# Ten spreading products cut into a product step and a read step, and gate and val converted in another order at the start

## Chip, cores and metric

One core of one Trainium2 chip runs the whole program. The metric is the device time of one execution in microseconds (us), the median over runs. Engines are called as in the profile: PE (TensorE, matmul), DVE (VectorE), ACT (ScalarE), POOL (GpSimd), SP (SyncE, which starts the DMAs here).

## What is computed

Attention of 4 x 8 heads over 576 positions with head size 64, where half of the heads look at the last 32 positions and half at every 32nd; then two feed-forward layers over the 2304 tokens. The inputs are float32, and the output is wanted to float32's accuracy.

```python
attn_out = _attn_ref(q, k, v)
x = attn_out.transpose(0, 2, 1, 3).reshape(B * S, H * D)   # 2304 x 512
h = x @ w_in                                               # 512 -> 2048
x = (h * np.cos(h)) @ w_out                                # 2048 -> 512
g = x @ w_gate                                             # 512 -> 1536
out = (g * (1.0 / (1.0 + np.exp(-g))) * (x @ w_val)) @ w_out2
```

## The kernel before

Every float32 matmul of the two layers is done as three float16 matmuls on a high and a low part of each operand (`mm3`, lines 559 to 561 in the profile). The parts are cut after the operand was multiplied by a scale that is common to a whole matrix or to a block of tokens. Weights arrive as 512 KB tiles of eight-byte words (`raw`, loaded from line 174 on SP's queue); ACT converts with line 233, DVE with lines 240 and 244, POOL joins with line 936 for the second layer's gate and val; then the high part is cut on ACT (line 254) and the low part on DVE (line 257), and finished tiles of the second layer are stored to DRAM (line 882).

A common scale takes three things. Partial maxima per partition are made while data passes by (lines 183 and 537). `spread_tops` (lines 120 to 137, DVE) makes of them a diagonal matrix, the `tops`. `common_scale` (lines 139 to 145) multiplies it on PE by a matrix of ones into a `bank` (line 142, the *spreading product*, 128 columns for each matrix or block), so that each partition sees all maxima, takes the maximum from the bank on DVE (line 143, the *read*) and makes the scale (lines 116 to 118). There are ten such products in an execution: for the matrices in, out, gate with val, and out2; for the first layer's input block 0, block 1, and blocks 2 to 4 together; and for the second layer's input block 0, blocks 1 to 3, and block 4.

A `bank` is one of four buffers in PSUM, which products and up-projections share; a new one is the buffer that was given back first.

The tokens are cut into five blocks, three of 512 and two of 384. The first layer runs in slots, one for each block and each of 16 tiles m of the hidden size. In a slot the program issues, in this order:

- PE: the up-projection of (block, m), twelve matmuls into a bank (`up1`), then the down-projections that are due, twelve matmuls each into four accumulators `acc` (`contract`). No down stands in the first 14 slots; later they catch up with the ups;
- ACT: the a step of this slot (line 592); DVE: the b step of the slot before (line 595);
- ACT and POOL finish an older slot's hidden tile (lines 606, 607);
- one piece of the `urgent` list (maxima, scales and splits of the token blocks);
- half of the slot's budget of `later` work (weights: maxima, tops, scales, conversions, each with a cost in us);
- ACT: the c step (line 599) and DVE: the d step (line 602), which reads the bank for the last time and so gives it back;
- the other half of the budget.

At the end of a block the accumulators are stored by ACT (line 575) and DVE (line 573) in `store_scaled`. Every engine works off its own instructions in the order in which the program issued them, so a step's place in the lists above decides what waits behind it. The steps that the change touches are put on the lists at these places: `scale_pieces` (token blocks, line 533 on), `direct_later` (matrix out), `open_weights` (gate with val, and out2, once enough of the hidden buffers are free), and `pair_half`, which sets the order of the conversions of gate and val. XM is the m of block 0 at which the urgent pieces of block 1 are listed.

Of the kernel before, what the change touches and what calls it, by code (L numbers as in the profile page):

```python
# [43 lines left out]
TW_IN = 2.0 ** 10  # L44
TW_OUT = 2.0 ** 14
TW_LAST = 2.0 ** 13
# [9 lines left out]
HEAD, HSHARE = 14, 0.8  # L56
RATE, MINLAG = 0.4, 2
RAW = 6
XM = 5
HOMES, LATE, UNIT, FREE = 24, 4, 16, 12  # L60
W7S = 3
SHARE, SHARE2, SB = 0.95, 0.85, 2
# [17 lines left out]
def build(tc, qk_l, qk_s, v_l, v_s, w_in, w_out, w_gate, w_val, w_out2, mask_l, mask_s, eye32, eye16, out):  # L80
    nc = tc.nc
    wide = w_in.dtype != F32
    with ExitStack() as ctx:
# [13 lines left out]
        ones16 = small.tile([128, 128], BF16, name="ones16")  # L97
# [9 lines left out]
        def brief(name, n=1):  # L107
            return small.tile([128, n], F32, name=f"{name}{n}", bufs=2)
# [27 lines left out]
                nc.vector.tensor_scalar(out=d[:, i], in0=id16, scalar1=p[:, i:i + 1], scalar2=None, op0=ALU.mult)  # L136
            return d

        def common_scale(d, bound, n=1):

            t, p = bank()[:, 0:128 * n].rearrange("p (n c) -> p n c", n=n), brief("q", n)
            nc.tensor.matmul(out=t, lhsT=ones16, rhs=d, start=True, stop=True)
            nc.vector.tensor_reduce(out=p, in_=t, op=ALU.max, axis=AX.X)
            s, inv = finish_scale(p, bound, n)
            return [(s[:, i:i + 1], inv[:, i:i + 1]) for i in range(n)]
# [14 lines left out]
        scale_w = {}  # L160
# [27 lines left out]
        def later(cost, fn, key=None):  # L188
            fill.append((cost, fn, key))
# [102 lines left out]
        tops = {}  # L292
# [3 lines left out]
            parts = parts_two if len(mats) == 2 else parts_w[mats[0]]  # L296
            later(0.6, lambda: tops.__setitem__(mats, spread_tops(parts, wide, len(mats))))

        def set_scales(bound, *mats):
            scale_w.update(zip(mats, common_scale(tops[mats], bound, len(mats))))  # L300

        def scale_later(bound, *mats):
            later(0.6, lambda: set_scales(bound, *mats))

        rests = deque()

        def direct_later(mat, j, tiles):

            box, steps = conv_steps(mat, j, lambda: ring.tile([128, 512], F32, name="cv", bufs=3), False)
            if rests:  # L310
                steps.append(rests.popleft())
            if j == 0:
                steps.append((0.6, lambda: set_scales(TW_OUT, mat)))
            steps.append((0, lambda: hi_part(tiles[j][:, 0], box["c"], scale_w[mat][0])))
            begin(steps)
            rests.append((0.7, lambda: lo_part(tiles[j][:, 1], box["c"], scale_w[mat][0], tiles[j][:, 0]), (mat, j)))
# [106 lines left out]
        def bank():  # L423
            return pm.tile([128, 512], F32, name="bank")
# [103 lines left out]
        def scale_pieces(blks, scales, at_once=1):  # L528
            n = len(blks)
            parts = cols("parts", n * (KC + 1)).rearrange("p (n k) -> p n k", n=n)  # L530
            box = {}
            nc.gpsimd.memset(parts[:, :, KC:], TINY)
            todo = [(i, k) for i in range(n) for k in range(KC)]

            def piece(some):
                for i, k in some:
                    nc.vector.tensor_reduce(out=parts[:, i, k:k + 1], in_=xy[blks[i]][:, k, :], op=ALU.max, axis=AX.X,
                                            apply_absolute_value=True)
            for i in range(0, len(todo), at_once):
                yield 0.65 * at_once, lambda some=todo[i:i + at_once]: piece(some)  # L540
            yield 0.6, lambda: box.__setitem__("top", spread_tops(parts if n > 1 else parts[:, 0], False, n))
            yield 0.6, lambda: scales.update(zip(blks, common_scale(box["top"], TX, n)))

        def split_pieces(blk, scales, dst):
# [235 lines left out]
                later(cost, fn)  # L780
        top_later("in")
        scan_later("out", 0)
        scale_later(TW_IN, "in")
        split_chain([("in", j, wi) for j in range(M1)], 2, lambda j: scan_later("out", j + 1) if j + 1 < M1 else top_later("out"))

        for i in range(2):
# [1 line left out]
        steps = deque()  # L788
# [5 lines left out]
        for k in range(len(gs) + LAGS[3] + 1):  # L794
            def group(lag):
                return gs[k - lag] if 0 <= k - lag < len(gs) else None
            i, g = 2 * (k // 6), k % 6
# [117 lines left out]
        def pair_half(j, mi, mat, last, ahead):  # L915
# [31 lines left out]

            g = [conv_steps(mat, 2 * j + q, lambda q=q: place(q), False)[1] for q in range(2)]
            his, los = ahead
            for step in (g[0][0:1] + los[0:1] + g[0][1:] + his[1:2] + g[1][0:1] + his[2:3] + g[1][1:2] + los[1:2] + g[1][2:]  # L950
                         + his[3:] + los[2:] + [(0, lambda k=k: combine(k)) for k in range(4)] + [(0, lambda: hi(0))]):
                if step:
                    later(*step)
            return [(0, lambda q=q: hi(q)) for q in range(3)], [(0.95, lambda q=q: lo(q)) for q in range(3)]

        def open_weights(lag):

            if lag + 4 <= FREE:
                most[0] = FREE
            if not opened and most[0] == FREE and max(taken, default=0) < FREE:  # L960
                opened.append(True)
                scale_later(TW_IN, "gate", "val")
                pairs_later()
                later(0, lambda: None, "pairs")
                for i in range(M2):
                    scan_later("out2", i, 0.8)
                top_later("out2")
            if len(opened) == 1 and lag < LATE and max(taken, default=0) < LATE:
                opened.append(True)
                most[0] = LATE  # L970
                for i in range(3):
                    later(1.0, lambda: None)
                scale_later(TW_LAST, "out2")
                seven_later()

        opened, most = [], [HOMES]
# [366 lines left out]
```

## Time and profile before

| what | value |
|---|---|
| runs, us | 881.54, 884.5, 879.95 (median 881.54) |
| the profiled execution | 880.38 us, span 878.6 us |
| mean granted TensorE clock | 0.992 |
| DVE busy | 658.8 us (75%) |
| ACT busy | 522.0 us (59%) |
| POOL busy | 202.5 us (23%) |
| DMA | 200.58 MB, 66.5% of 16 engines' span on the main queue |

The span runs from the first to the last instruction of the profiled execution, and its time has 1.8 us around it. Busy time counts an instruction from its start to its (for PE: modelled) end. The attention takes about the first 112 us with the first weights beside it, the first layer runs to about 500 us, the second to the end. The spreading products run at 63.8, 86.3, 131.1, 139.0, 217.0, 243.9, 381.0, 414.1, 485.4 and 648.7 us.

### The profile page before, as it was taken

What the parts mean: (1) busy time and instruction counts of PE and PEld (TensorE: products, weight loads), DVE (VectorE), ACT (ScalarE), POOL (GpSimd) and SP (SyncE); (2) the same over time, 40 slices, a digit from 0 to 9 for tenths busy, and PEclk for the clock granted to TensorE, in tenths of its full rate; (3) what the DMA queues carried; (4) which work ended last, traced back from release to release, by engine and by line L of the source; (5) the groups of instructions that cost most, each with busy time, mean ns of one, the idle gap of its engine ahead of it and who ended that gap; (6) DMA issues with size and microseconds to landing.
All of it is one profiled execution on the core that took longest, in us unless ns stands there. A gap on an engine that the chain in (4) does not pass through costs nothing.

```text
span 878.6 us, 18390 instructions
## 1 busy us (share of the span) xinstructions
PE 851.0 (97%) x7223; PEld 604.9 (69%) x7223; DVE 658.8 (75%) x1256; ACT 522.0 (59%) x1046; POOL 202.5 (23%) x249
## 2 busy tenths in 40 slices
PE   7999999999999999999999998999999999999998
PEld 4776644444444444455656687888888899999998
DVE  5898989995788989979997378657766765765562
ACT  4888989762556767567886365554444534544440
POOL 3343324221245567323223100000000000000000
PEclk8899999999999999999999999999999999999999
DMA  9998842566855565734546147576777778898894
GB/s 296 358 312 256 268 166 73 167 191 241 288 179 186 175 213 206 257 151 136 198 147 226 69 168 275 195 263 226 264 244 249 250 241 282 296 321 296 321 326 157
DMA packets 53510, 200.58 MB, mean 228 GB/s; under 512 B 5456, under 2 KB 16208, under 8 KB 49584
## 3 DMA queue, kind: packets, MB, share of 16 engines
q1 hardware_dynamic: 53424, 199.42, 66.5%
q8 instruction: 56, 0.92, 0.4%
q14 instruction: 30, 0.25, 0.1%
HBM read 175.41 MB, written 23.99 MB: 227 GB/s over the span
## 4 chain that ended last, share of the span: by engine, by line
PE 74%; issue 6%; POOL 6%; DVE 5%; DMA 4%; ACT 4%; SPq 0%; POOLq 0%; ACTq 0%; DVEq 0%
PE acc L712 14%; PE bank L559 12%; PE bank L561 11%; PE bank L560 11%; PE acc L559 6%; PE acc L561 6%; PE acc L560 6%; POOL arena L936 3%; PE bank L448 2%; POOL arena L607 2%; PE po L501 2%; DMA vl<-v_l 1%; DMA v_pair<-v_s 1%; DVE arena L257 1%; ACT tb L592 1%
## 5 line engine op out<-in xcount | busy, mean ns | idle before, releaser
L559 PE MATMUL bank<-xs,wi 128*128 128x256 f16 (+3 forms) x780 | 232.6, 298 | 12.2 <-DVE tb L602 7.2
L561 PE MATMUL bank<-xs,wi 128*128 128x256 f16 (+3 forms) x780 | 232.6, 298 | 0.0
L560 PE MATMUL bank<-xs,wi 128*128 128x256 f16 (+3 forms) x780 | 232.6, 298 | 0.0
L607 POOL TENSOR_TENSOR arena<-tb,arena 128x512 f16<-128x512 f32 (+1 forms) x80 | 94.1, 1176 | 234.0 <-ACT arena L606 213.8
L560 PEld LDWEIGHTS <-wi 128*128 128x128 f16 x880 | 86.0, 98 | 51.3 <-issue 17.9
L559 PE MATMUL acc<-arena 128*128 128x512 f16 (+1 forms) x320 | 114.5, 358 | 0.0
L560 PE MATMUL acc<-arena 128*128 128x512 f16 (+1 forms) x320 | 114.5, 358 | 0.0
L561 PE MATMUL acc<-arena 128*128 128x512 f16 (+1 forms) x320 | 114.5, 358 | 0.0
L559 PEld LDWEIGHTS <-wi 128*128 128x128 f16 x880 | 86.1, 98 | 35.1
L561 PEld LDWEIGHTS <-wi 128*128 128x128 f16 x880 | 86.1, 98 | 34.8
L712 PEld LDWEIGHTS <-arena 128*128 128x128 f16 x1080 | 100.7, 98 | 8.1
L697 POOL TENSOR_TENSOR wi<-tb 128x256 f32<-128x256 f32 (+1 forms) x30 | 20.2, 673 | 341.7 <-DVE tb L679 341.7
L679 DVE SCALAR_TENSOR_TENSOR tb<-tb,c,arena 128x512 f32<-128x512 f32 (+1 forms) x60 | 41.6, 693 | 63.5 <-ACT tb L674 63.4
L560 PEld LDWEIGHTS <-arena 128*128 128x128 f16 x600 | 58.7, 98 | 34.1 <-issue 1.4
L712 PE MATMUL acc<-arena 128*128 128x256 f16 (+1 forms) x702 | 82.0, 265 | 0.0
L561 PEld LDWEIGHTS <-arena 128*128 128x128 f16 x600 | 58.7, 98 | 32.8
L559 PEld LDWEIGHTS <-arena 128*128 128x128 f16 x600 | 58.7, 98 | 32.6
L592 ACT ACTIVATE tb<-bank,quarter,c 128x512 int32<-128x512 f32 (+1 forms) x75 | 54.4, 725 | 39.0 <-PE bank L561 28.2
L682 ACT ACTIVATE arena<-tb 128x256 f16<-128x256 f32 (+3 forms) x59 | 28.9, 489 | 79.7 <-DVE tb L679 79.7
L1211 DVE TENSOR_TENSOR arena<-bank,cv 128x512 f32<-128x512 f32 (+1 forms) x60 | 38.1, 635 | 45.8 <-PE bank L561 45.2
L606 ACT ACTIVATE arena<-tb 128x512 f16<-128x512 f32 (+1 forms) x80 | 46.6, 583 | 37.6 <-PE acc L561 35.1
L559 PE MATMUL bank<-xs,arena 128*128 128x256 f16 (+1 forms) x240 | 62.9, 262 | 1.2 <-DVE arena L1211 1.2
(144 smaller groups left out, 1711.9 us busy)
## 6 DMA issues: line engine op xcount, KB each, us to landing
wi<-w SPq DMA_DIRECT2D x20, 1792.0 KB
arena<-w SPq DMA_DIRECT2D x60, 576.0 KB, 5.2
raw<-w_out SPq DMA_DIRECT2D x56, 512.0 KB, 4.3
arena<-w SPq DMA_DIRECT2D x10, 1792.0 KB
raw<-w_gate SPq DMA_DIRECT2D x24, 512.0 KB, 4.1
raw<-w_val SPq DMA_DIRECT2D x24, 512.0 KB, 4.8
w<-arena SPq DMA_DIRECT2D x42, 256.0 KB, 2.8
raw<-w_in SPq DMA_DIRECT2D x16, 512.0 KB
```

The costliest lines, as they stand in the source:

```text
L559: nc.tensor.matmul(out=o, lhsT=w[:, 0, c], rhs=x[0], start=first, stop=False, **kw)
L560: nc.tensor.matmul(out=o, lhsT=w[:, 0, c], rhs=x[1], start=False, stop=False, **kw)
L561: nc.tensor.matmul(out=o, lhsT=w[:, 1, c], rhs=x[0], start=False, stop=last, **kw)
L592: nc.scalar.activation(out=c["w"].bitcast(I32), in_=c["ph"], func=AF.Identity, scale=turn[c["blk"]], bias=quarter)
L606: nc.scalar.activation(out=g[:, 0, 0:n], in_=w, func=AF.Copy)
L607: nc.gpsimd.tensor_tensor(out=g[:, 1, 0:n], in0=w, in1=g[:, 0, 0:n], op=ALU.subtract)
L679: nc.vector.scalar_tensor_tensor(out=t, in0=t, scalar=s_g[c["blk"]], in1=c["C"][m][:, 1, 0:c["n"]], op0=ALU.mult, op1=ALU.mult)
L682: nc.scalar.activation(out=to, in_=src, func=AF.Copy, scale=2.0 ** -11)
L697: nc.gpsimd.tensor_tensor(out=t_sums[:, 0, 0:h], in0=c["t"][0][:, h:2 * h], in1=c["t"][0][:, 0:h], op=ALU.subtract)
L712: nc.tensor.matmul(out=o[:, c], lhsT=w[:, 256 * i + 128 * c:256 * i + 128 * c + 128], rhs=unit(u)[:, x:x + h], start=j == c == i == 0, sto ...
L936: nc.gpsimd.tensor_tensor(out=out, in0=a, in1=b, op=op)
L1211: nc.vector.tensor_tensor(out=c["C"][m][:, :, h * right:h * right + h], in0=p, in1=t, op=ALU.add)
```

## The change

`common_scale` loses its product, which becomes `spread_product`. Where a scale was one step of a list (product and read together, cost 0.6), there are now two: the product at cost 0, then, as the next step of the list, the read with the scale at cost 0.6. For the urgent list, which gives one piece to a slot, that is the next slot. For out2 the three empty steps of cost 1.0 ahead of the scale become one ahead of the product and two between product and read. For gate and val the step leaves `open_weights`; the product is issued first in the conversions of the first half pair, whose conversions follow it at once, and the read stands behind the first conversions of the second half. XM goes from 5 to 4, and the list of block 1 has one step more.

```diff
--- before.py
+++ after.py
@@ -56,7 +56,7 @@
 HEAD, HSHARE = 14, 0.8
 RATE, MINLAG = 0.4, 2
 RAW = 6
-XM = 5
+XM = 4
 HOMES, LATE, UNIT, FREE = 24, 4, 16, 12
 W7S = 3
 SHARE, SHARE2, SB = 0.95, 0.85, 2
@@ -136,10 +136,13 @@
                 nc.vector.tensor_scalar(out=d[:, i], in0=id16, scalar1=p[:, i:i + 1], scalar2=None, op0=ALU.mult)
             return d
 
-        def common_scale(d, bound, n=1):
-
-            t, p = bank()[:, 0:128 * n].rearrange("p (n c) -> p n c", n=n), brief("q", n)
+        def spread_product(d, n=1):
+            t = bank()[:, 0:128 * n].rearrange("p (n c) -> p n c", n=n)
             nc.tensor.matmul(out=t, lhsT=ones16, rhs=d, start=True, stop=True)
+            return t
+
+        def common_scale(t, bound, n=1):
+            p = brief("q", n)
             nc.vector.tensor_reduce(out=p, in_=t, op=ALU.max, axis=AX.X)
             s, inv = finish_scale(p, bound, n)
             return [(s[:, i:i + 1], inv[:, i:i + 1]) for i in range(n)]
@@ -296,11 +299,11 @@
             parts = parts_two if len(mats) == 2 else parts_w[mats[0]]
             later(0.6, lambda: tops.__setitem__(mats, spread_tops(parts, wide, len(mats))))
 
-        def set_scales(bound, *mats):
-            scale_w.update(zip(mats, common_scale(tops[mats], bound, len(mats))))
-
-        def scale_later(bound, *mats):
-            later(0.6, lambda: set_scales(bound, *mats))
+        def product_step(*mats):
+            return 0, lambda: tops.__setitem__(mats, spread_product(tops[mats], len(mats)))
+
+        def scale_step(bound, *mats):
+            return 0.6, lambda: scale_w.update(zip(mats, common_scale(tops[mats], bound, len(mats))))
 
         rests = deque()
 
@@ -310,7 +313,8 @@
             if rests:
                 steps.append(rests.popleft())
             if j == 0:
-                steps.append((0.6, lambda: set_scales(TW_OUT, mat)))
+                steps[1:1] = [product_step(mat)]
+                steps.append(scale_step(TW_OUT, mat))
             steps.append((0, lambda: hi_part(tiles[j][:, 0], box["c"], scale_w[mat][0])))
             begin(steps)
             rests.append((0.7, lambda: lo_part(tiles[j][:, 1], box["c"], scale_w[mat][0], tiles[j][:, 0]), (mat, j)))
@@ -539,6 +543,7 @@
             for i in range(0, len(todo), at_once):
                 yield 0.65 * at_once, lambda some=todo[i:i + at_once]: piece(some)
             yield 0.6, lambda: box.__setitem__("top", spread_tops(parts if n > 1 else parts[:, 0], False, n))
+            yield 0, lambda: box.__setitem__("top", spread_product(box["top"], n))
             yield 0.6, lambda: scales.update(zip(blks, common_scale(box["top"], TX, n)))
 
         def split_pieces(blk, scales, dst):
@@ -780,7 +785,8 @@
                 later(cost, fn)
         top_later("in")
         scan_later("out", 0)
-        scale_later(TW_IN, "in")
+        later(*product_step("in"))
+        later(*scale_step(TW_IN, "in"))
         split_chain([("in", j, wi) for j in range(M1)], 2, lambda j: scan_later("out", j + 1) if j + 1 < M1 else top_later("out"))
 
         for i in range(2):
@@ -947,6 +953,16 @@
 
             g = [conv_steps(mat, 2 * j + q, lambda q=q: place(q), False)[1] for q in range(2)]
             his, los = ahead
+            if j == 0:
+                first = g[0] + g[1] + [(0, lambda k=k: combine(k)) for k in range(4)]
+                if mi == 0:
+                    for step in [product_step("gate", "val")] + first:
+                        later(*step)
+                    return [(0, lambda q=q: hi(q)) for q in range(3)], [(0.95, lambda q=q: lo(q)) for q in range(3)]
+                for step in (g[0] + [scale_step(TW_IN, "gate", "val")] + his[0:1] + g[1][0:1] + his[1:2] + g[1][1:2] + los[0:1]
+                             + his[2:3] + g[1][2:] + los[1:2] + first[len(g[0]) + len(g[1]):] + [(0, lambda: hi(0))] + los[2:]):
+                    later(*step)
+                return [(0, lambda q=q: hi(q)) for q in range(3)], [(0.95, lambda q=q: lo(q)) for q in range(3)]
             for step in (g[0][0:1] + los[0:1] + g[0][1:] + his[1:2] + g[1][0:1] + his[2:3] + g[1][1:2] + los[1:2] + g[1][2:]
                          + his[3:] + los[2:] + [(0, lambda k=k: combine(k)) for k in range(4)] + [(0, lambda: hi(0))]):
                 if step:
@@ -959,7 +975,6 @@
                 most[0] = FREE
             if not opened and most[0] == FREE and max(taken, default=0) < FREE:
                 opened.append(True)
-                scale_later(TW_IN, "gate", "val")
                 pairs_later()
                 later(0, lambda: None, "pairs")
                 for i in range(M2):
@@ -968,9 +983,11 @@
             if len(opened) == 1 and lag < LATE and max(taken, default=0) < LATE:
                 opened.append(True)
                 most[0] = LATE
-                for i in range(3):
+                later(1.0, lambda: None)
+                later(*product_step("out2"))
+                for i in range(2):
                     later(1.0, lambda: None)
-                scale_later(TW_LAST, "out2")
+                later(*scale_step(TW_LAST, "out2"))
                 seven_later()
 
         opened, most = [], [HOMES]
```

Behind the change's added lines, line 142 becomes 141, 143 becomes 146, 183 becomes 186, 240 and 244 become 243 and 247, 257 becomes 260, 559 to 561 become 564 to 566, 573 becomes 578, 595 becomes 600 and 602 becomes 607.

On PE, the product of out2 in the first layer's block 3, where the downs of the block before end. Before, the downs of `acc_3754` are followed by the up at once (wi is its weights), and the product comes some 50 rows later:

```order
L560 MATMUL acc_3754<-arena 128x512
L561 LDWEIGHTS arena
L561 MATMUL acc_3754<-arena 128x512
L559 LDWEIGHTS wi
L559 MATMUL bank<-xs,wi 128x384
L560 LDWEIGHTS wi
L560 MATMUL bank<-xs,wi 128x384
```

and

```order
L560 MATMUL acc_4464<-arena 128x384
L561 LDWEIGHTS arena
L561 MATMUL acc_4464<-arena 128x384
L142 LDWEIGHTS ones_77
L142 MATMUL bank<-tops,ones_77 128x128
L559 LDWEIGHTS wi
L559 MATMUL bank<-xs,wi 128x384
```

Of the change:

```order
L565 MATMUL acc_3754<-arena 128x512
L566 LDWEIGHTS arena
L566 MATMUL acc_3754<-arena 128x512
L141 LDWEIGHTS ones_77
L141 MATMUL bank<-tops,ones_77 128x128
L564 LDWEIGHTS wi
L564 MATMUL bank<-xs,wi 128x384
L565 LDWEIGHTS wi
L565 MATMUL bank<-xs,wi 128x384
```

The product has moved ahead of the up with its downs, one slot earlier.

On DVE in the same place, of the change (L578 stores the accumulators, L600 is the b step, L260 a split of the tokens, L124 to L136 make the tops, L607 is the d step):

```order
L578 TENSOR_SCALAR xy_68<-acc_3752,c_3757 128x512
L578 TENSOR_SCALAR xy_68<-acc_3754,c_3757 128x512
L600 SCALAR_TENSOR_TENSOR tb<-bank,c_4227,tb 128x384
L260 SCALAR_TENSOR_TENSOR xs<-xy_70,s_3090,xs 128x384
L124 TENSOR_REDUCE m_4438<-pw_out_81 128x1
L127 TENSOR_SCALAR a_4441<-m_4438 128x1
L129 SCALAR_TENSOR_TENSOR p_4439<-m_4438,a_4441 128x1
L136 TENSOR_SCALAR tops<-id_76,p_4439 128x128
L607 SCALAR_TENSOR_TENSOR tb<-tb,bank 128x384
```

These rows stand in the same order before; only the product on PE has moved against them.

On DVE, the read for blocks 2 to 4 (`q`, 128x3), before:

```order
L595 SCALAR_TENSOR_TENSOR tb<-bank,c_2527,tb 128x512
L143 TENSOR_REDUCE q_3042<-bank 128x3
L116 RECIPROCAL s_3045<-q_3042 128x3
L117 TENSOR_SCALAR inv_3046<-q_3042 128x3
L118 TENSOR_SCALAR s_3045<-s_3045 128x3
L183 TENSOR_REDUCE pw_two<-raw 128x1
L602 SCALAR_TENSOR_TENSOR tb<-tb,bank 128x512
L183 TENSOR_REDUCE pw_two<-raw 128x1 x2
L573 TENSOR_SCALAR xy_66<-acc_2484,c_2489 128x512
L573 TENSOR_SCALAR xy_66<-acc_2486,c_2489 128x512
L595 SCALAR_TENSOR_TENSOR tb<-bank,c_2527,tb 128x512
L183 TENSOR_REDUCE pw_two<-raw 128x1
```

and of the change:

```order
L600 SCALAR_TENSOR_TENSOR tb<-bank,c_2527,tb 128x512
L186 TENSOR_REDUCE pw_two<-raw 128x1 x2
L607 SCALAR_TENSOR_TENSOR tb<-tb,bank 128x512
L186 TENSOR_REDUCE pw_two<-raw 128x1
L578 TENSOR_SCALAR xy_66<-acc_2484,c_2489 128x512
L578 TENSOR_SCALAR xy_66<-acc_2486,c_2489 128x512
L600 SCALAR_TENSOR_TENSOR tb<-bank,c_2527,tb 128x512
L146 TENSOR_REDUCE q_3088<-bank 128x3
L116 RECIPROCAL s_3090<-q_3088 128x3
L117 TENSOR_SCALAR inv_3091<-q_3088 128x3
L118 TENSOR_SCALAR s_3090<-s_3090 128x3
L186 TENSOR_REDUCE pw_two<-raw 128x1
```

The read and its three small instructions have moved behind both stores (L573, now L578) and the next b step.

On DVE, the read for gate and val (`q`, 128x2), before:

```order
L124 TENSOR_REDUCE m_3258<-pw_two 128x2
L127 TENSOR_SCALAR a_3261<-m_3258 128x2
L129 SCALAR_TENSOR_TENSOR p_3259<-m_3258,a_3261 128x2
L136 TENSOR_SCALAR tops_3264<-id_76,p_3259 128x128 x2
L143 TENSOR_REDUCE q_3268<-bank 128x2
L116 RECIPROCAL s_3271<-q_3268 128x2
L117 TENSOR_SCALAR inv_3272<-q_3268 128x2
L118 TENSOR_SCALAR s_3271<-s_3271 128x2
L240 TENSOR_SCALAR arena<-arena 128x512
L244 SCALAR_TENSOR_TENSOR arena<-raw,arena 128x512
L602 SCALAR_TENSOR_TENSOR tb<-tb,bank 128x512
```

and of the change:

```order
L600 SCALAR_TENSOR_TENSOR tb<-bank,c_2527,tb 128x512
L260 SCALAR_TENSOR_TENSOR xs<-xy_68,s_3090,xs 128x512
L243 TENSOR_SCALAR arena<-arena 128x512
L247 SCALAR_TENSOR_TENSOR arena<-raw,arena 128x512
L243 TENSOR_SCALAR arena<-arena 128x512
L247 SCALAR_TENSOR_TENSOR arena<-raw,arena 128x512
L607 SCALAR_TENSOR_TENSOR tb<-tb,bank 128x512
L243 TENSOR_SCALAR arena<-arena 128x512
L247 SCALAR_TENSOR_TENSOR arena<-raw,arena 128x512
L146 TENSOR_REDUCE q_3288<-bank 128x2
```

Ahead of the read now stand three pairs of conversions (L243, L247) and the b and d steps of a slot; the tops are made earlier, ahead of these rows.

## Rows read from the trace of the kernel before

**Rows 1.** The page's table of engines: busy us, share of the span, instructions.

```profile
PE 851.0 (97%) x7223; PEld 604.9 (69%) x7223; DVE 658.8 (75%) x1256; ACT 522.0 (59%) x1046; POOL 202.5 (23%) x249
```

**Rows 2.** The list of waits: engine, tile, line, releaser: total us, times, longest.

```profile
DVE q L143 <- PE bank L142: 20.9, 5, 8.8
...
PE bank L559 <- DVE tb L602: 7.2, 9, 1.7
```

**Rows 3.** Timeline of PE, 217 to 223.3 us: start, duration, form [idle <-releaser].

```profile
217.04 0.33 PE L142 MATMUL bank<-tops,ones 128*128 128x384 bf16 x1
218.01 0.38 PE L559 MATMUL bank<-xs,wi 128*128 128x512 f16 x1 [0.65 <-DVE q L143]
...
223.19 0.38 PE L559 MATMUL bank<-xs,wi 128*128 128x512 f16 x1
```

**Rows 4.** Timeline of DVE, 217 to 225 us.

```profile
217.40 0.56 DVE L143 TENSOR_REDUCE q<-bank 128x3 f32<-128x384 f32 x1 [8.79 <-PE bank L142]
...
223.39 0.75 DVE L573 TENSOR_SCALAR xy<-acc,c 128x512 f32<-128x512 f32 x1 [0.54 <-PE acc L561]
...
224.72 0.68 DVE L183 TENSOR_REDUCE pw_two<-raw 128x1 f32<-128x512 f32 x1
```

**Rows 5.** Timeline of PE, 377 to 383 us.

```profile
377.04 0.33 PE L559 MATMUL bank<-xs,wi 128*128 128x384 f16 x1
...
380.99 0.22 PE L142 MATMUL bank<-tops,ones 128*128 128x128 bf16 x1
382.88 0.32 PE L559 MATMUL bank<-xs,wi 128*128 128x384 f16 x1 [1.67 <-DVE tb L602]
```

**Rows 6.** Timeline of DVE, 377 to 382.8 us.

```profile
377.25 0.75 DVE L573 TENSOR_SCALAR xy<-acc,c 128x512 f32<-128x512 f32 x1 [0.54 <-PE acc L561]
...
378.44 1.29 DVE L257 SCALAR_TENSOR_TENSOR xs<-xy,s,xs 128x384 f16<-128x384 f32 x1
...
380.39 0.55 DVE L602 SCALAR_TENSOR_TENSOR tb<-tb,bank 128x384 f32<-128x384 f32 x1
...
381.75 0.61 DVE L257 SCALAR_TENSOR_TENSOR xs<-xy,s,xs 128x384 f16<-128x384 f32 x1
382.28 0.55 DVE L602 SCALAR_TENSOR_TENSOR tb<-tb,bank 128x384 f32<-128x384 f32 x1
```

**Rows 7.** Timeline of PE at 244.7 and at 414.7 us.

```profile
244.70 0.38 PE L559 MATMUL bank<-xs,wi 128*128 128x512 f16 x1 [0.52 <-DVE q L143]
...
414.68 0.32 PE L559 MATMUL bank<-xs,wi 128*128 128x384 f16 x1 [0.38 <-DVE q L143]
```

**Rows 8.** Timeline of ACT at 240.8 and of DVE from 245 us.

```profile
240.80 0.65 ACT L233 ACTIVATE arena<-raw 128x512 f32<-128x512 f32 x1
...
244.96 0.42 DVE L240 TENSOR_SCALAR arena<-arena 128x512 int32<-128x512 int32 x1
245.41 0.69 DVE L244 SCALAR_TENSOR_TENSOR arena<-raw,arena 128x512 int32<-128x512 int32 x1
246.02 0.68 DVE L602 SCALAR_TENSOR_TENSOR tb<-tb,bank 128x512 f32<-128x512 f32 x1
```

**Rows 9.** Timeline of DVE, 412.9 to 416 us.

```profile
412.89 0.60 DVE L595 SCALAR_TENSOR_TENSOR tb<-bank,c,tb 128x384 f32<-128x384 f32 x1
...
414.93 0.42 DVE L336 TENSOR_TENSOR arena<-raw,arena 128x256 f32<-128x256 f32 x1
...
415.73 0.94 DVE L257 SCALAR_TENSOR_TENSOR arena<-raw,s,arena 128x512 f16<-128x512 f32 x1
```

**Rows 10.** PE at 14.5; stretches: busy PE, PEld, DVE, ACT, POOL; PEclk.

```profile
14.48 0.33 PE L483 MATMUL tp<-id,e_s 128*128 128x128 f32 x1 [3.88 <-POOL e_s L472]
...
12.00:16.00 4.00, 1.52 (x16) 1.03 (x16) 0.52 (x2) 1.07 (x6) 1.25 (x3) 0.89 1.03 416
24.00:28.00 4.00, 4.00 (x41) 2.75 (x42) 2.69 (x8) 2.58 (x9) 1.53 (x3) 0.50 1.03 408
28.00:32.00 4.00, 4.00 (x61) 2.92 (x61) 2.67 (x7) 3.64 (x14) 1.64 (x3) 0.90 1.02 400
```


## Prediction

> **What bounds the kernel now.** The first view is the page's table of engines: TensorE (PE) is busy for 97% of the span, VectorE (DVE) for 75% [rows 1]. So time is won or lost only where PE stands still, and the change moves work between PE's and DVE's places in the program without taking any away. The second view, the list of waits, says what the change is aimed at: DVE waits 20.9 us in five places for the spreading product (line 142), 8.8 us in the worst [rows 2]. That is idle time of an engine which is not the bound; it costs something only if PE later waits for what DVE would have done meanwhile. The third view, the timeline of PE, is therefore the one that counts: where does an up-projection (line 559) start late, and which DVE instruction ended its wait? The list of waits gives 7.2 us in nine waits for the d step (line 602, which gives a bank back) [rows 2]; the timelines around five of the ten products show the rest. The fourth view is the order of the instructions before and after (in the part on the change), which says who now stands ahead of whom.
>
> One fact about the banks carries most of the sum. There are four, and the program hands out the one that was given back first. A product is a user of a bank like an up-projection is. When the product at 217.04 took one, the next up stood until 218.01 for the read of line 143 that began at 217.40 and ran 0.56 us [rows 3, 4]: 217.96, and PE went on 0.05 us later. So a product whose read comes a slot later holds one of the four banks for a slot longer.
>
> **The change part by part.** The number of products, reads, matmuls and conversions stays the same; what is added as "a step" has no instruction of its own. No DMA is added; the conversions' loads and stores on SP's queue follow their conversions, and PE's stalls in this stretch end with DVE's line 602 or 143, not with a transfer. On PE the order shows only two products that move, that of block 1 and that of out2, each one slot earlier. Of the ten reads on DVE, five move behind work of the next slot. I take the places in the order of time.
>
> *A, block 1's scale, about 136 us.* Its product stands one slot earlier, and an extra step is made up for by beginning at m = 4. Below I take 0 us: PE has no wait here in the timeline before. Above I take 0.8 us, the mean of a wait for line 602, 7.2 us over 9 [rows 2]. I choose +0.2, near the lower end, since the tops belong to a single block here and little DVE work stands ahead of them.
>
> *B, scales of blocks 2 to 4, 217 us.* The up at 218.01 no longer waits for the read: the product at 217.04 needs one matmul's place of about 0.16, so that up could begin at 217.20, and 0.81 us are won [rows 3]. But the read now stands behind both stores of line 573 and the b step of line 595 (see the order rows). The second store begins at 223.39, after the accumulator of the last down-projection; then comes the b step, and what follows both begins at 224.72 [rows 4]. The read goes there: 224.72 + 0.56 = 225.28. The up that took its bank at 223.19 in the run before [rows 3] now gets the product's bank, because one more is out; it can begin at about 225.33, 2.14 us late. Net 2.14 - 0.81 = **+1.3 us**, between 1.2 and 1.5. Behind the waiting PE stand that slot's downs; DVE's next d step and ScalarE wait with it, and lose nothing of their own. The Trainium skill's "Perfetto Trace Analysis", section "Optimizing Tensor Performance", wants independent matmul groups to rotate through different PSUM banks so that the emptying of one overlaps the next group; by that rule alone the split is a gain, here 0.81 us. The trace supports the rule only with a bank to spare, and by rows 3 and 4 none is left two ups later.
>
> *C, scales of gate and val, 244 us.* The up at 244.70 waited 0.52 us for the read [rows 7], a hole of 0.68 against the cadence of the matmuls; that is the most to be won. The conversions now come first on DVE, then the d step for which the up will wait. ScalarE's part of the first conversion ends at 240.80 + 0.65 = 241.45 [rows 8]; two pairs of lines 240 and 244 (0.42 + 0.69 each) and the d step (0.68) take 2.90 [rows 8], so 244.35 against 244.70: **-0.35 us** (0 to -0.68). The 6.3 us of DVE idle before this read are filled with conversions, but I cost that at nothing else: in the following slots DVE waits again for PE's accumulators, so a conversion done earlier does not make an up start earlier.
>
> *E, scale of out2, 377 us: the largest term.* Before, the product stood behind the downs and ran at 380.99 [rows 5]. Now it stands ahead of the up that began at 377.04 [rows 5], and PE takes its instructions in order: the up, and the downs behind it, wait until the tops are there. These come at the end of a chain on DVE which starts at 377.25 with the store of line 573, then the b step, then a split of line 257 that took 1.29 us [rows 6], then the four small instructions of the tops, then the d step at 380.39 + 0.55 = 380.94 [rows 6]. The built program makes the up behind the product wait for exactly that d step. It begins at about 380.99 in place of 377.04: +3.95 us. Given back is the wait of the up after it. From the up at 377.04 to the end of its downs, where the product stood, PE worked 3.95 us [rows 5]; begun at 380.99, that ends at 384.94. The next up needs the d step that ended at 382.83 [rows 6], which does not hang on the late up, so it starts at 384.94 without a wait, where before it waited and started at 382.88 [rows 5]. Net 384.94 - 382.88 = **+2.1 us**. The lower bound is 1.4, if the split takes 0.61 as the next one does [rows 6]; the upper is 3.95, if nothing is given back.
>
> *F, first scale for the second part, 414 us.* The up at 414.68 waited for the read, 0.38 us [rows 7]; now it waits for the d step of that slot. The b step ends at 412.89 + 0.60 = 413.49; then come an addition of line 336 (0.42), a split of line 257 (0.94) and the d step (0.55) [rows 6, 9]. Back to back by their durations that is 415.40, +0.7; instructions start before their predecessors' ends in these rows by some 0.1 each, and the split often takes less, so I take 415.0: **+0.3 us** (0 to +0.7).
>
> The reads at 485 and 649 us move too, but the timeline has PE in its downs there, with no up waiting for the read: 0.
>
> **Sum:** 0.2 + 1.3 - 0.35 + 2.1 + 0.3 = +3.55 us. The profiled execution took 880.38, so 883.9 against it. It lies 1.16 us under the median of the three runs, 881.54; against the median the forecast is **885.1 us**, 0.4% more. By the ends of the terms (0 + 1.2 - 0.68 + 1.4 + 0 = 1.9, and 0.8 + 1.5 + 0 + 3.95 + 0.7 = 7.0) it lies between 883.4 and 888.5.
>
> **The rivals.** *The holes close and nothing opens.* If the tops of out2 and the bank at 223 us came in time, only the gains would be left: -0.81 at 218, -0.68 at 244, -0.38 at 414, together -1.9: 879.7. For it: DVE's 20.9 us of idle [rows 2] is room to do the reads early. Against it: the order puts the late store ahead of one read and the tops' chain ahead of one product, and both chains have times. Chance 0.13.
>
> *The late ups are absorbed.* PE is held up elsewhere for several us by DVE and ScalarE; if those waits shrink by what was lost, the time stays at 881.5. Against it: those engines are fed by PE in the same loop and shift with it. Chance 0.2.
>
> *The clock falls at 380 us.* This is the one that decides the sign. Before 14.48 PE stood for 3.88 us, and then the granted clock was 0.50 (1.2 GHz) in place of 1.00 (2.4 GHz): the stretches 12 to 16, 24 to 28 and 28 to 32 us have 0.89, 0.50 and 0.90 [rows 10], which puts the half clock between about 15.1 and 28.8. E makes PE stand for about 3.9 us. If the same happens there, one up of twelve matmuls loses its own 1.95 us (887.0), and 13.7 us at half speed lose 6.8 us (891.9). For it: the length of the stand is that of the row. Against it: PE is full on both sides of it here and was not there, and other stands of under 2 us had no such effect; if the split is short, the stand is 3.3 us. The point from which it decides is whether the clock falls at all. The Trainium skill's "TensorE: Matmul & The Clock Gate", section "Part 1: The HAM clock gate (the "warmup" mystery)", says the throttled clock is the default and activity releases it; rows 10 agree. By that page an idle stretch could bring it back. Chance 0.17.
>
> **How the numbers follow.** Forecast 0.5, holes closed 0.13, absorbed 0.2, clock 0.17. A measurement of this kernel tells about 0.5%, 4.4 us, from no change: faster is below 877.1, slower above 885.95. No case reaches 877.1; I keep 0.05 for gains that I do not see. Slower: half of the clock's cases lie well above and the other half at 887.0, so 0.17, and 0.16 of the forecast's half, whose middle is 0.85 under the bound. That is 0.33; same has the rest, 0.62. The range goes from 879.7 (holes closed) to 888.5 (the forecast's own upper end, with the mild fall of the clock); the forecast's own range is 883.4 to 888.5.
>
> **What would show it.** Right: a wait of nearly 4 us of PE at the out2 product, and the wait at 382.88 gone; an up five or six us after the product of blocks 2 to 4 that waits some 2 us for the read; no hole right behind the products at 217 and 244. Wrong: E's product running within 1 us of the down before it; the up at 223 starting at once; a clock under 1.0 between 380 and 395; or new waits of PE in the conversions from 245 to 375, which would say that their new order counts and I left it out.

## The result and the profile after

The changed kernel takes **888.57 us** (median of 7 runs, 886.93 to 894.55) against 882.21 before in the same comparison; the ratio is 1.0077, with a 95% interval of 1.0049 to 1.0104. It is slower: the medians differ by 6.4 us and the ratio makes about 6.8, where 3.55 were forecast. The profiled execution took 888.57, its span is 886.6 us, its mean granted clock 0.987 in place of 0.992.

The list of waits of the changed kernel (engine, tile, line <- releaser: total us, times, longest):

```profile
PE bank L564 <- DVE tb L607: 7.3, 11, 1.5
...
PE bank L141 <- DVE tops L136: 4.3, 3, 3.3
```

DVE's wait for the product, 20.9 us in [rows 2], is down to 0.3 us in the full list. In its place PE, the engine that bounds the kernel, waits for the tops: 3.3 us at one product.

The timeline of PE of the changed kernel (start, duration, line, form [idle before <- releaser]):

```profile
137.46 0.22 PE L141 MATMUL bank<-tops,ones 128*128 128x128 bf16 x1 [0.42 <-DVE tops L136]
138.06 0.38 PE L564 MATMUL bank<-xs,wi 128*128 128x512 f16 x1 [0.38 <-DVE tb L607]
...
225.82 0.38 PE L564 MATMUL bank<-xs,wi 128*128 128x512 f16 x1 [1.97 <-DVE q L146]
...
246.99 0.38 PE L564 MATMUL bank<-xs,wi 128*128 128x512 f16 x1 [0.18 <-DVE tb L607]
...
379.40 0.38 PE L566 MATMUL acc<-arena 128*128 128x512 f16 x1
383.10 0.27 PE L141 MATMUL bank<-tops,ones 128*128 128x128 bf16 x1 [3.32 <-DVE tops L136]
383.56 0.48 PE L564 MATMUL bank<-xs,wi 128*128 128x384 f16 x1 [0.20 <-DVE tb L607]
...
384.15 0.52 PE L566 MATMUL bank<-xs,wi 128*128 128x384 f16 x1
384.47 0.52 PE L564 MATMUL bank<-xs,wi 128*128 128x384 f16 x1
...
422.65 0.32 PE L564 MATMUL bank<-xs,wi 128*128 128x384 f16 x1 [0.90 <-DVE tb L607]
```

Against [rows 3, 5, 7]: the up right behind the product of blocks 2 to 4 does not wait any more, but the one at 225.82 waits 1.97 for the read; gate and val's wait is 0.18 in place of 0.52; out2's product waits 3.32 for its tops, the up behind it another 0.20; the up at 422.65 waits 0.90 in place of 0.38. New are two waits at 137 us. And the matmuls of 384 columns at 384.15 start 0.32 apart, where the same form started 0.16 apart before.

The timeline of DVE of the changed kernel at the two late places:

```profile
223.89 0.75 DVE L578 TENSOR_SCALAR xy<-acc,c 128x512 f32<-128x512 f32 x1 [0.55 <-PE acc L566]
224.56 0.74 DVE L600 SCALAR_TENSOR_TENSOR tb<-bank,c,tb 128x512 f32<-128x512 f32 x1
225.22 0.55 DVE L146 TENSOR_REDUCE q<-bank 128x3 f32<-128x384 f32 x1
...
381.01 1.29 DVE L260 SCALAR_TENSOR_TENSOR xs<-xy,s,xs 128x384 f16<-128x384 f32 x1
...
382.79 0.25 DVE L136 TENSOR_SCALAR tops<-id,p 128x128 bf16<-128x128 bf16 x1
382.96 0.55 DVE L607 SCALAR_TENSOR_TENSOR tb<-tb,bank 128x384 f32<-128x384 f32 x1
```

The read at 225.22 stands behind the store and the b step; the tops end at 382.79 + 0.25 = 383.04, and the product starts 0.06 us later.

The view by stretches of the changed kernel (us, busy PE, PEld, DVE, ACT, POOL, granted clock, DMA share, GB/s):

```profile
380.00:382.00 2.00, 0.00 (x0) 0.00 (x0) 2.00 (x3) 1.83 (x4) 0.91 (x1) 1.00 1.01 408
382.00:384.00 2.00, 0.71 (x3) 0.36 (x3) 1.86 (x9) 0.00 (x0) 0.00 (x0) 0.65 0.83 330
384.00:386.00 2.00, 2.00 (x8) 0.88 (x6) 1.95 (x7) 0.00 (x0) 0.00 (x0) 0.50 0.07 23
386.00:388.00 2.00, 2.00 (x8) 0.89 (x7) 0.00 (x0) 0.34 (x1) 0.00 (x0) 0.50 0.00 0
388.00:390.00 2.00, 2.00 (x9) 1.02 (x8) 0.62 (x1) 0.33 (x1) 0.00 (x0) 0.64 0.00 0
390.00:392.00 2.00, 2.00 (x15) 1.22 (x13) 0.41 (x1) 1.47 (x3) 0.80 (x1) 1.00 0.00 0
```

A stretch of 2 us with a mean clock of 0.65 holds 1.4 us at the half clock, if only 0.50 and 1.00 occur. So the half clock lasted 1.4 + 4 + 1.44 = 6.8 us, from about 382.6, before PE's stand ended, to about 389.4. Before, every stretch behind 120 us has 1.00.

**Where the 8.0 us of the two profiled spans lie.** The start of the same ACT instruction (the a step) in both traces gives the lateness along the way:

| place | lateness before and behind it, us | change |
|---|---|---|
| attention, to the first up-projection (113.00 / 113.52) | 0 to 0.52 | +0.52 |
| A, 137 to 150 us | 0.52 to 1.32 | +0.80 |
| B, 218 to 226 | 1.31 to 2.63 | +1.32 |
| C, 245 | 2.63 to 2.28 | -0.35 |
| a wait at 366 that is longer than before | 2.29 to 2.57 | +0.28 |
| E, 379 to 390 | 2.57 to 7.45 | +4.88 |
| F, 422 | 7.45 to 7.97 | +0.52 |
| to the end | 7.97 to 7.99 | 0 |

E's 4.88 are the stand, 3.49 + 0.40 beyond the matmuls' cadence (the steady time from one start to the next), less the 1.84 us wait at the next up, which is gone: 2.05; the other 2.83 come from the half clock.

### The profile page after: what moved, and what is told of

Same layout as the page of the kernel before. It is cut to its first block, busy times and chain, and to the rows that moved or that the text cites. A ratio compares the mean times of both kernels' runs of the same rounds, so it can differ in the third digit from the quotient of the medians.

```text
span 886.6 us, 18389 instructions
## 1 busy us (share of the span) xinstructions
PE 856.2 (97%) x7223; PEld 606.9 (68%) x7223; DVE 657.5 (74%) x1256; ACT 521.8 (59%) x1046; POOL 201.2 (23%) x249
## 4 chain that ended last, share of the span: by engine, by line
PE 73%; DVE 9%; issue 6%; POOL 5%; ACT 3%; DMA 3%; POOLq 0%; ACTq 0%; DVEq 0%
PE acc L717 14%; PE bank L564 12%; PE bank L566 11%; PE bank L565 11%; PE acc L564 6%; PE acc L566 6%; PE acc L565 6%; POOL arena L942 3%; PE bank L452 2%; PE po L505 2%; POOL arena L612 2%; DMA v_pair<-v_s 1%; DMA vl<-v_l 1%; DVE arena L260 1%; PE tp L483 1%
```

## Experiments

The attention ahead of the first up-projection took between 112.6 and 118.5 us in the profiled executions of these kernels, with half-clock stretches of other lengths, whatever the kernel. So the experiments are read from the first up-projection behind the attention to the end (one up already stands inside it), and from single waits; the ratio to before, from all runs, stands beside.

| kernel | ratio to before (95%) | first up at, us | from there to the end | half clock at out2, us |
|---|---|---|---|---|
| before | 1 | 113.00 | 765.60 | 0 |
| changed | 1.0077 (1.0049 to 1.0104) | 113.52 | 773.07 | 6.8 |
| out2_back | 1.0036 (1.0000 to 1.0073) | 118.45 | 768.20 | 0 |
| out2_alone | 1.0015 (0.9987 to 1.0044) | 114.01 | 770.17 | 6.8 |
| out2_fill16 | 1.0050 (1.0000 to 1.0101) | 117.12 | 770.20 | 0 |
| out2_fill8 | 1.0053 (1.0028 to 1.0077) | 113.60 | 771.50 | 0 |
| three_back | 1.0036 (1.0012 to 1.0059) | 113.26 | 769.87 | 3.4 |
| blk1_back | 1.0053 (1.0026 to 1.0080) | 113.98 | 772.06 | 6.8 |
| after_again | 1.0078 (1.0050 to 1.0105) | 114.65 | 774.27 | 6.8 |
| best3 | 0.9961 (0.9929 to 0.9993) | 113.10 | 764.75 | 0 |
| best4 | 0.9950 (0.9929 to 0.9972) | 112.57 | 762.70 | 0 |
| best7 | 0.9964 (0.9938 to 0.9990) | 114.96 | 762.17 | 0 |

### out2_back: out2's product where it stood before

```diff
-                later(1.0, lambda: None)
-                later(*product_step("out2"))
-                for i in range(2):
+                for i in range(3):
                     later(1.0, lambda: None)
+                later(*product_step("out2"))
                 later(*scale_step(TW_LAST, "out2"))
```

> The change with one part undone: the product of out2 stands where it stood before (three empty steps, then product and read together). Theory (PE standing 3.9 us for the tops lets the clock fall, and both cost): no PE wait of 3.5 us at 379 to 383, granted clock 1.00 from 380 to 400 us, and 4.9 us less than the changed kernel: 883.7 us, about 1.002 of before. Rival (the clock falls there for another reason, for instance the DMA load or the work of the other engines): the standing goes, 2.0 us are won, 886.5 us, and the clock of 380 to 400 us stays near 0.83.

Stretches and PE's timeline of this kernel:

```profile
376.00:384.00 8.00, 8.00 (x44) 4.17 (x43) 6.45 (x12) 4.23 (x8) 2.08 (x2) 1.00 1.01 406
384.00:392.00 8.00, 6.33 (x39) 3.63 (x38) 7.27 (x20) 4.87 (x9) 2.25 (x2) 1.00 0.62 249
...
388.51 0.22 PE L141 MATMUL bank<-tops,ones 128*128 128x128 bf16 x1
390.40 0.32 PE L564 MATMUL bank<-xs,wi 128*128 128x384 f16 x1 [1.67 <-DVE tb L607]
```

The clock is 1.00, the stand is gone and the old wait of 1.67 is back. From the first up on it takes 768.20, 4.87 less than the changed kernel; 4.9 were expected.

### out2_alone: that part alone, in the kernel before

```diff
-                for i in range(3):
+                later(1.0, lambda: None)
+                later(0, lambda: tops.__setitem__(("out2",), spread_product(tops["out2",])))
+                for i in range(2):
                     later(1.0, lambda: None)
-                scale_later(TW_LAST, "out2")
+                later(0.6, lambda: scale_w.update(zip(["out2"], read_scale(tops["out2",], TW_LAST))))
```

> The kernel before with one part of the change alone: the product of out2 after one empty step, its read after two more. Theory: PE stands 3.9 us at 377 to 381, the wait of 1.8 us at the next up goes, the granted clock falls to 0.50 for about 6.7 us; 4.9 us more than before: 887.0 us. Rival (the fall needs what the other parts of the change shift, so that the standing meets it at another moment): clock 1.00, only 2.0 us more: 884.2 us.

```profile
376.00:384.00 8.00, 4.48 (x19) 1.95 (x18) 6.73 (x16) 3.35 (x6) 0.92 (x1) 0.77 0.81 325
384.00:392.00 8.00, 8.00 (x41) 4.41 (x40) 1.99 (x6) 2.88 (x5) 0.92 (x1) 0.80 0.00 0
```

The wait for the tops is again 3.49 beyond the cadence, the clock falls, and the rest of the program takes 4.57 us more than before, where the rival has 2.0. Over its ten runs the ratio is only 1.0015, and 4.57 us (1.0052) lie above the end of its interval; the attention scatters by more than that between runs, but how often the loss is smaller than in the profile stays open.

### out2_fill16 and out2_fill8: the same wait, but PE works in it

```diff
-        def spread_product(d, n=1):
-            t = bank()[:, 0:128 * n].rearrange("p (n c) -> p n c", n=n)
+        def spread_product(d, n=1, fill=0):
+            b = bank()
+            for i in range(fill):
+                nc.tensor.matmul(out=b, lhsT=wi[0][:, 0, 0:128], rhs=wi[0][:, 0, :], start=True, stop=True)
+            t = b[:, 0:128 * n].rearrange("p (n c) -> p n c", n=n)
```

with `fill` 16 or 8 for out2 alone. The extra matmuls are not part of the computation; the product overwrites them.

> The changed kernel with 16 extra matmuls of 128x512 ahead of the out2 product, into the product's own bank, on weights that are long there: PE works 3.4 us of the time for which it waits for the tops. The product and the up behind it can't come earlier. Theory (the standing lets the clock fall): the product still starts at about 383.1 us, but the granted clock stays 1.00, and the 2.8 us that the half clock took come back: 885.7 us. Rival (the clock does not hang on this wait): clock 0.83 in 380 to 400 us as in the changed kernel, 888.6 us.

> The changed kernel with 8 extra matmuls of 128x512 ahead of the out2 product: PE works 1.7 us of its wait and stands about 2 us of it. Judged from the first up-projection to the end, since the attention ahead of it differs from run to run (765.6 us before, 773.1 the changed kernel, 770.2 with 16 extra matmuls). Theory: a stand of about 2 us does not lower the clock, as at 382.88 us before: clock 1.00 from 380 to 400 us and 770.2 us. Rival (any wait for the tops lowers it, and the 16 matmuls only just hid it): clock near 0.9 or lower there, 771.5 to 773 us.

With 16, PE's timeline and two stretches:

```profile
383.23 3.62 PE L142 MATMUL bank<-wi 128*128 128x512 f16 x16
386.72 0.22 PE L144 MATMUL bank<-tops,ones 128*128 128x128 bf16 x1
387.18 0.32 PE L567 MATMUL bank<-xs,wi 128*128 128x384 f16 x1 [0.25 <-DVE tb L610]
...
376.00:384.00 8.00, 8.00 (x42) 3.96 (x41) 6.00 (x10) 4.11 (x8) 1.20 (x2) 1.00 1.00 394
384.00:392.00 8.00, 7.75 (x45) 4.20 (x43) 6.05 (x18) 2.85 (x7) 0.97 (x2) 1.00 0.46 185
```

The up behind the product starts as late as ever, 3.95 us after the filling began, but the clock stays 1.00 and 2.87 us come back. This separates the two costs: about 2.05 for the stand, 2.8 for the clock. The separation rests on one profile of this kernel and one of the next; the ratios, 1.0050 and 1.0053 against 1.0077, have intervals that overlap.

With 8:

```profile
381.21 1.89 PE L142 MATMUL bank<-wi 128*128 128x512 f16 x8
384.70 0.22 PE L144 MATMUL bank<-tops,ones 128*128 128x128 bf16 x1 [1.60 <-DVE tops L136]
...
224.00:232.00 8.00, 6.09 (x21) 2.46 (x21) 7.93 (x17) 3.65 (x7) 1.44 (x2) 0.79 0.40 130
376.00:384.00 8.00, 7.10 (x36) 3.43 (x35) 6.55 (x11) 4.89 (x9) 1.83 (x2) 1.00 1.02 412
384.00:392.00 8.00, 7.06 (x44) 4.22 (x44) 4.99 (x15) 2.88 (x5) 0.92 (x1) 1.00 0.19 77
```

At out2 the clock is 1.00 with 1.60 us of idle left, as the theory has it. The total is 1.3 us above the expected 770.2 nevertheless, and the first row shows why: in this execution the clock fell behind the 2.13 us wait at 226 us (B), to a mean of 0.79 in 224 to 232; counted from the first up, the ups behind it are 1.7 us later than in the changed kernel's profile.

### three_back: blocks 2 to 4 in one step again

```diff
+            if blks == [2, 3, 4]:
+                yield 0.6, lambda: scales.update(zip(blks, common_scale(spread_product(box["top"], n), TX, n)))
+                return
             yield 0, lambda: box.__setitem__("top", spread_product(box["top"], n))
```

> The change with one part undone: product and read of blocks 2 to 4 are one step again. Theory (a bank held for a slot longer makes the up two slots on wait): the wait of 2.1 us before the up at 225.8 goes, one of 0.8 us comes back right behind the product, 1.3 us less: 887.2 us. Rival (the up at 225.8 is late because the block's stores stand on DVE, not because of the read): it stays late by about 2 us and the time is above 888.6.

```profile
218.10 0.33 PE L141 MATMUL bank<-tops,ones 128*128 128x384 bf16 x1
219.07 0.38 PE L567 MATMUL bank<-xs,wi 128*128 128x512 f16 x1 [0.65 <-DVE q L146]
...
224.00:232.00 8.00, 8.00 (x38) 3.63 (x37) 7.51 (x14) 5.53 (x9) 2.33 (x2) 1.00 0.78 271
376.00:384.00 8.00, 4.43 (x17) 1.91 (x16) 6.75 (x18) 3.15 (x6) 0.92 (x1) 0.84 0.75 300
380.00:382.00 2.00, 0.73 (x3) 0.35 (x3) 1.86 (x9) 0.00 (x0) 0.00 (x0) 0.88 0.87 350
381.03 0.22 PE L141 MATMUL bank<-tops,ones 128*128 128x128 bf16 x1 [3.33 <-DVE tops L136]
...
384.00:392.00 8.00, 8.00 (x48) 4.71 (x47) 1.55 (x2) 3.71 (x7) 1.09 (x2) 0.94 0.00 0
```

The wait right behind the product is back (0.65, as in [rows 3]) and the later one is gone, with PE busy for all of 224 to 232. The rest of the program takes 3.2 us less, not 1.3. By the starts of the a step and of the ups, B gives 1.3 of it, as expected, and the clock 1.2: the half clock at out2 lasted 3.4 us here, from about 381.5, and E costs 3.70 in place of 4.88. Gate and val's wait goes altogether, 0.3 more than in the changed kernel; DVE's d step stands ahead of the second conversion's line 247 there. The rest are shorter waits at 364 and 419 us.

### blk1_back: block 1 in one step again, from m = 5

The edit is that of three_back with `blks == [1]`, and XM = 5.

> The change with one part undone: block 1's product and read are one step and begin at m = 5 again. Judged by PE's waits from 130 to 150 us and the lateness of the up-projections behind them. Theory: the two waits at 137.5 and 138.1 us (0.59 and 0.54) go, the one of 0.34 at 149.7 comes back, 0.8 us less than the changed kernel at 150 us; the rest as in the changed kernel, with a half clock of 3 to 7 us at 383. Rival (the lateness comes from the read of the out matrix, which also moved): the waits stay.

```profile
127.49 0.23 PE L141 MATMUL bank<-tops,ones 128*128 128x128 bf16 x1 [0.40 <-DVE tops L136]
127.56 0.38 PE L567 MATMUL bank<-xs,wi 128*128 128x512 f16 x1
```

The waits at 137 and 138 are gone, but one of 0.40 stands at 127.49, in front of the product of the matrix out. In the changed kernel this product has not moved on PE: before and in the changed kernel it runs 18.1 us behind the first up (113.00 and 113.52) and waits for nothing:

```profile
131.12 0.22 PE L142 MATMUL bank<-tops,ones 128*128 128x128 bf16 x1
...
131.64 0.22 PE L141 MATMUL bank<-tops,ones 128*128 128x128 bf16 x1
```

In blk1_back it runs 13.5 us behind the first up, two ups earlier. So this run brings a wait that the changed kernel does not have, and its lateness at 150 us is 0.33 in place of 0.80, not 0. The changed kernel's 0.80 are its own two waits (0.59 and 0.54 beyond the cadence) less the 0.34 at 149.7 (0.17 of it idle) that it no longer has. The wait at 137.46 is block 1's: its tops end it. The one at 138.06 is ended by a d step, and two things can make it: block 1's product takes a bank a slot earlier, and the read of out gives its bank back 25.1 us behind the first up in place of 21.0. blk1_back undoes both (21.3), so the rival is not settled for this wait.

### after_again: the changed kernel once more

> The changed kernel unaltered, once more. Theory: the waits are those of the program and come out the same (2.13 us at the up after the read of blocks 2 to 4, 3.49 and 0.40 at out2), while the half clock's length is not the program's: 773.1 us from the first up-projection to the end with 6.7 us of half clock in the first profile, between 771 and 774 here. Rival (the length belongs to this kernel): 6.7 us of half clock and 773.1 us again.

```profile
220.00:250.00 30.00, 27.86 (x122) 12.13 (x120) 18.62 (x37) 12.54 (x20) 5.36 (x5) 0.94 0.46 166
376.00:384.00 8.00, 6.33 (x33) 3.02 (x31) 6.46 (x11) 4.51 (x9) 1.40 (x2) 1.00 1.02 417
384.00:392.00 8.00, 6.16 (x20) 2.86 (x20) 4.97 (x16) 1.05 (x2) 0.43 (x1) 0.57 0.35 136
```

The waits are the same to 0.02 us (2.13 at the late up, 3.49 and 0.40 at out2). The half clock at out2 is 6.8 us again, as in four of the five profiles with that stand; the fifth has 3.4. So on the length the rival was right, and 774.27 lies just above the 774 that I had set as the end: twice the same kernel, twice 6.8 us. The 3.4 stand in another kernel, three_back, and what sets the length stays open. Here the clock fell behind B as well (mean 0.94 in 220 to 250), which costs 1.7 us; F and the wait at 366 are 0.2 to 0.3 us shorter, which leaves 1.2 us above the first profile.

### best3, best4 and best7: what is left if the costs are taken out

best3 undoes the split for block 1, for the second layer's block 0 and for out2, and begins the list of blocks 2 to 4 one slot earlier; best4 puts one more empty step ahead of out2's product; best7 also puts the product of out back. The lines that undo block 1 and block 0, which are like those of three_back, and XM = 5 are not shown.

```diff
-                if m == (2 if blk else XM) and blk + 1 < NBLK:
+                if m == (1 if blk == 1 else 2 if blk else XM) and blk + 1 < NBLK:
...
-                for i in range(3):
+                for i in range(4):
                     later(1.0, lambda: None)
                 later(*product_step("out2"))
...
-                steps[1:1] = [product_step(mat)]
+                steps.append(product_step(mat))
```

> The change without what cost: product and read of block 1 and of the second part's block 0 are one step again, out2's product and read stand where they stood before, and the list of blocks 2 to 4 begins one slot earlier (m = 1), so that its late read no longer stands behind the stores. What is kept is the split for blocks 2 to 4 and the new order for gate and val. Theory, from the first up-projection to the end: 765.6 - 0.81 (hole behind the product at 217) - 0.35 (gate and val) = 764.4 us, clock 1.00 throughout. Rival (the bank that the product of blocks 2 to 4 holds costs a wait wherever its read stands a slot later): 765.3 or more.

> As best3, with four empty steps ahead of out2's product in place of three: its product stands one slot later than before, after the stores of the block. Theory: DVE is no longer behind there, so the up after the product does not wait for the d step, and the 1.8 us of PE's wait at 382.88 go: 762.6 us from the first up-projection to the end, 3 us under the kernel before. Rival (the wait is that of a block's first slots, product or not): 764.4 us, with the wait still there.

> As best4, and the product of the matrix out goes back beside its read's slot: it stood one slot earlier in all the runs so far that did not undo it, and PE waited 0.57 us for its tops at 127 us in the run with block 1 undone. Theory: that wait goes, 0.4 us less than best4: 762.3 us from the first up-projection to the end. Rival (the hole comes back as a wait of an up behind it, as at 149.7 us before): 762.7 us, no gain.

best3 takes 764.75, 0.85 less than before; 1.16 were expected. That it comes so near is in part luck: the product of out stands two ups earlier, as in blk1_back, and costs 0.35, a wait at 363 us is 0.27 longer, and gate and val give 0.67 in place of 0.35. It has no wait at all behind the products at 212 and 243 us: a product that is read in time costs nothing, so the bank is only dear where the read is late. In best4 the product of out2 stands behind the stores, and nothing waits:

```profile
383.60 0.22 PE L141 MATMUL bank<-tops,ones 128*128 128x128 bf16 x1
383.66 0.33 PE L567 MATMUL bank<-xs,wi 128*128 128x384 f16 x1
```

762.70, 2.05 less than best3. What was expected of best7 takes out's product to have stood a slot earlier in all the runs; it stood earlier only in those with block 1 undone (blk1_back, best3, best4). best7's wait at 127 is gone and the one of 0.17 at 149.7 us of before is back, as both sides had it; the time from the first up is 762.17, 3.4 us under the kernel before. By the ratios best4 and best7 are both 0.4 to 0.5% faster than before and not told apart.

## Why the prediction was wrong

The direction and the places were right, the sum was too small, and the time lies just above the range.

- **The step that failed** is the choice in "The clock falls at 380 us": I gave this rival 0.17 and forecast a clock of 1.00, with the argument that PE is full on both sides of the stand. That argument is refuted. In all five profiles with PE idle for more than 3 us at out2 (changed, after_again, out2_alone, three_back, blk1_back) the clock fell within the stand or, in three_back, 0.5 us behind its end; in none of the others did it fall there. Row for row, the length of the stand was the right thing to read in [rows 10], and what PE had done earlier was not. The price, 2.83 us in the changed kernel, lies between that rival's two values, 2.0 and 6.8: the half clock lasted 6.8 us and not the 13.7 of the attention's. Over the five profiles the price is 1.6 to 2.8 us (E's lateness less the 2.05 of the stand), the least in three_back. The Trainium skill's page "TensorE: Matmul & The Clock Gate", section "Part 1: The HAM clock gate (the "warmup" mystery)", has the clock fall after idling, and these five agree.
- **E without the clock** was right: the product at the tops' end, 3.89 us of stand for 3.95, the wait at the next up gone, net 2.05 for 2.1. out2_fill16 shows this part by itself: 770.20, which is 773.07 less the clock's 2.87.
- **B** was right in place and size: +1.32 for +1.3, the wait two ups on, 2.13 for 2.14; three_back removes it. What was left out is that such a stand can lower the clock too: it did in two of the six profiles that have it (out2_fill8 and after_again).
- **C** was right: -0.35 for -0.35. In three_back and best3 the whole hole goes (0.67), near the far end that I gave.
- **A** was mis-sized: 0.80 for 0.2, at the upper end that I gave. I expected little DVE work ahead of block 1's tops; PE was idle for 0.42 us until they came, and for 0.38 until a d step behind them. That only block 1's and out2's products move on PE was right. Of the reads I missed one: that of the matrix out comes 4.1 us later, and whether the wait for the d step is its doing or block 1's is not shown.
- **F** was mis-sized: 0.52 for 0.3 (0.3 in after_again), within its bounds. The other rivals fell: the late ups were not absorbed anywhere, lateness stays at 7.97 to 7.99 us over the last 460 us.

With the clock's 2.83 and A's 0.6 added to the forecast's 3.55, the sum is 7.0; the measured ratio makes 6.8 of 882.21. That the time lies so near the range is luck: the upper end, 888.5, holds E's 3.95 with nothing given back, which did not come. Of the signs of being wrong that I named, the clock under 1.0 came. The wait at 366 us, 0.28 longer, can't be put down to the new order: in after_again, the same kernel, PE is idle for 0.92 us there, as before.

## What to carry to other kernels

Moving a small matmul ahead of independent work pays only if its operand is ready at its new place: an in-order engine makes everything behind it wait, so look up when the operand's last instruction ends before moving. A read that is put off holds its buffer, and what stands ahead of it on the reading engine in the next slot (here a block's stores) decides what that costs. Where PE is made to stand for as long as at out2 (3.3 us of idle), add the half clock to the price, here 1.6 to 2.8 us. Matmuls that nobody reads kept the clock up in the two runs that put them into the stand; the stand itself they did not shorten.

## What the runs showed of the hardware

The granted clock fell in five of five stands of 3.3 us at out2, in two of six of 2.0 us at 226, and behind none of the shorter ones after 120 us in all twelve profiles (up to 1.7 us of idle). The half clock then lasted 6.8 us in four and 3.4 us in one of the first group, and 3.4 us in both of the second (out2_fill8 and after_again); in the attention it lasted 13.7 us before. That the stand at 226 us ends differently in two profiles of the same program (the changed kernel and after_again) was not expected, and why is open. With eight and with sixteen matmuls of 512 columns ahead of the wait, the clock stayed at 1.00 at out2, in one profile each.
